# One written-out order of all five engines replaced by another in a kernel of chunk-selecting attention and a gated MLP

## The chip, the core and the metric

The kernel runs on one core of a Trainium2 chip. The metric is the device time of one execution in microseconds (us). A core has TensorE (PE: products into PSUM, one queue of weight loads and products), VectorE (DVE), ScalarE (ACT), GpSimd (POOL) and SyncE (SP); here POOL issues the loads from memory and SP issues the transfers inside the core and the stores. All of them run at once and meet only at semaphores; each works through its own instructions in the order in which they were written.

## What is computed

Four batches of eight heads, 768 positions, 64 numbers a head. Keys are cut into 24 chunks of 32 positions; a query attends to the six chunks whose bound (from the chunk's smallest and largest key) is highest.

```
ub = sum(max(q*k_min, q*k_max))            # per query and chunk, causal
sel = the 6 chunks with the largest ub
attn = softmax(scale * q @ k.T, where sel and j <= i)
x = (attn @ v), heads side by side         # 4 x 768 x 512
h = relu(x @ w_in);  u, v = halves of h
v_n = (v - mean) / sqrt(var + 1e-6)
out = (u * (w_spatial @ v_n + b_spatial)) @ w_out
```

## The kernel before

**Pairs.** The work of the attention is cut into 16 pairs of heads, four to a batch; two pairs share one group g of loads. For pair i the operations carry these names: `lk`, `lq`, `lv` (POOL starts the loads of keys, queries and values, L598, L604, L609; for group 0 in quarters, L613), `kT` (six TensorE transposes of the keys, L674), `kmax`, `kmin` (DVE, chunk bounds, L698), `kb` (L725), `qT` (five transposes of the queries, L739), `rq` (positive and negative parts, L748, L750; the very first on ACT, L745), `ub` (bounds on TensorE, L756, L759), `top` (ten maxima on DVE, L769), `sel` (which chunks fall out, L795; it writes into the query tile `qs`, beside the queries, whose other columns were zeroed by `ring`, L541). The query tile is then transposed into the tile `a`: for pairs 0 to 7 on TensorE (`aT`, L802 and L814, with copies `ac`, L807 to L817), for pairs 8 to 15 by a DMA transpose that SP issues (`aTd`, L820). The tile `kh` holds the transposed keys and the matrix that spreads a chunk's mask over its 32 positions (`kh`, L583); `kop` brings the keys there: copies on ACT or DVE for pairs 0 to 7 (L734), DMAs issued by SP for pairs 8 to 15 (L732), one for each head of the pair; `kc` (L720) is the copy out of PSUM before them. `kop91` is thus the DMA for the second head of pair 9.

**Scores to output.** `sc` (scores, six groups of up to 512 columns for each head, L827), `ex` (exponential on ACT, L836), `tri` (the causal triangle on POOL for batches 1 to 3, L842), `av` (L853), `rc` and `nm` (division, L858, L863), then the transpose of the result `x` into the layout of the MLP: through TensorE (`xp`, L878, and a copy, L881) for pairs 0 to 3 and 15, by an SP DMA transpose (L872) for the others. `sc901` is pair 9, first head, group 1; `sc914` pair 9, second head, group 4.

**MLP.** For each batch and each of six blocks of 128 positions: `v` and `u` (products with `w_in`), `va`, `bs`, `vs`, `rs`, `vn` (normalising), `s` (product with `w_spatial`), `gt` (L994), `gd` (DMA transpose of the gated block by SP, L1009; the last two through TensorE, L1001), `o` (product with `w_out`), `oc` (copy, L1014), `os` (store by SP, L1018). All these products are line L951. Those of one batch are put between the pairs of the next.

**Zero products.** `dm` (L889) multiplies a tile of zeros: 42 products at the start, then single ones (`dm0` to `dm64`) placed among the first pairs.

**What sets the order.** A planner in the file (`build`, L171) knows each operation's engine, duration, inputs and buffers. What it found was written into the file as one string `ORDER` (L393 to L465) of 1452 names; the kernel walks through it (L1054) and emits each operation on its engine. So the order on each engine is the order of the names of that engine's operations, and nothing is rearranged later. `PLAN` (L391) holds the counts of buffers, the number of zero products and a list `flip` of the copies that change between ACT and DVE. A semaphore wait stands on the instruction that needs the data, and whatever follows it on that engine waits too. POOL's DMAs share eight semaphores in turn, SP's another eight, so that a DMA isn't issued before the one eight places earlier has landed.

**Counting a place.** TensorE starts a 128-column product 0.056 us after the one before it, a 512-column one 0.216 us after (104 of them in a row took 22.48 us in the chain of waits). With every product counted at such a spacing and without the zero products, the kernel has 177.0 us of TensorE work; "the place" of a name is the work that stands ahead of it in `ORDER`. The first scores are at place 3.2, the first product of the MLP (`v00.0`) at 32.7.

Of the kernel before, what the change touches and what calls it, by code (L numbers as in the profile page):

```python
# [166 lines left out]
def mmc(n): return max(n/2.4+2.5,25)/1000  # L167
DEF=dict(BEATS=12,pa=8,dve_a=(),qx=('ACT',),xp=4,mlp_first=13,mlp_mul=1.0,sc=3,tr=1,acc=1,ml=3,kbuf=3,qbuf=3,vbuf=3,ebuf=3,late=240,chunk=2,
  lk=40,lq=36,lv=18,kdma=99,kcp=2,kcdma=1,kc_act=(),shift=4,prep=0.0,tm=.8,lm=0.2,lm2=1.2,gp=(),head=1,lag=0.0,kp=27,ca=99,tree=0,svk=1.48,svh=.96,svw=1.15,flip=(),wide=0,pt=(),kdm=0,xd=(),dum=0,dum0=42,split=1,warm0=0.,qa_dve=(),ma_act=(),mkbuf=2)
PEL=0.2  # L170
def build(prm=None):  # L171
# [8 lines left out]
    for i in range(p['qbuf']): op(f'ring{i}','DVE',.81,.05,deps=['id0'],prio=B0 if i==0 else B0+.9)  # L180
# [210 lines left out]
PLAN = {'late': 40, 'mlp_first': 8, 'qbuf': 5, 'kbuf': 6, 'vbuf': 6, 'dum': 65, 'warm0': 5.3, 'kcp': 8, 'flip': ['ac10', 'ac41', 'ac51', 'ac60', 'ac71', 'gd34', 'kc10', 'kc12', 'kc13', 'kc9', 'kh00', 'kh11', 'kop00', 'kop40', 'kop71', 'oc01', 'oc03', 'oc13', 'oc21'], 'gp': ((3, 4), (3, 5)), 'lm': 0.2, 'lm2': 1.2, 'tm': 0.8, 'dum0': 42, 'split': 1}  # L391

ORDER = """  # L393
dz id0 dm ring3 lk010 ring2 lk000 ring0 lq010 id1 lq000 expand lk001 kh00 kh30 ring4 lk011 kT0 kh21 ring1 mlat dm0
kTb0 lq011 dm1 kh11 dm2 dm3 dm4 dm5 kop01 dm6 dm7 kmin0 dm8 dm9 dm10 dm11 lq001 qTb0 kh31 qT0 kmax0 dm12 lk11 dm13
dm14 dm15 dm16 dm17 dm18 dm19 dm20 rq01 dm21 dm22 dm23 dm24 small dm25 dm26 dm27 dm28 dm29 dm30 lk10 kh20 kb0 kT1 rq00
kop00 ub0 kh01 lv0 dm31 dm32 kmax1 kTb1 dm33 dm34 kop11 qT1 top00 lq10 dm35 dm36 dm37 dm38 dm39 kmin1 dm40 dm41 kop10
dm42 dm43 dm44 dm45 dm46 dm47 dm48 dm49 dm50 dm51 mtri dm52 dm53 dm54 selA0 dm55 kh10 top01 aTA00 lq11 dm56 kb1 dm57
dm58 dm59 sel0 rq11 aTB0 dm60 rq10 dm61 dm62 dm63 dm64 wsp0 acA00 ub1 win00 acB0 sc000 top10 sc001 lk20 ex000 aTA01
top11 sc002 ex001 acA01 sc005 kT2 lk21 sel1 ex002 sc004 kop20 ex005 sc013 ex004 lq20 sc011 kmin2 ex013 aT10 sc003  # L400
ex011 sc010 ac10 lq21 av000 ex003 kop21 aT11 ex010 sc015 av001 lv1 sc100 kmax2 ex015 av002 ac11 sc012 rc00 kb2 ex012
qT2 nm00 sc102 lk31 ex100 kT3 rq21 av010 ex102 rq20 sc014 win21 kmax3 sc112 ex014 ub2 win11 sc101 ex112 kmin3 sc104
qT3 ex101 sc111 av011 ex104 top20 lk30 sc105 av012 ex111 kb3 sc103 top21 ex105 rc01 sc113 sel2 ex103 rq31 wsp4 aT20
ex113 rq30 sc115 sc114 ac20 nm01 ub3 kop30 ex114 av100 win01 sc201 ex115 top30 av101 ex201 sc203 kop31 av102 sc110
ex203 lv2 top31 ex110 aT21 rc10 sel3 kT4 ac21 nm10 qT4 sc200 kmin4 sc205 sc202 ex200 aT30 kmax4 ex202 sc215 av110
ex205 ex215 wsp5 av111 rq40 kop40 sc211 av112 kb4 rq41 sc204 sc212 ex211 rc11 kop41 ub4 lq30 aT31 ac30 sc210 top40 kT5
ex204 nm11 xp0 lq31 ex212 top41 av200 kop50 ac31 sc213 win30 av201 sel4 ex210 av202 sc214 kmax5 qT5 ex213 win20 sc300
ex214 xp1 rc20 rq51 sc301 ex300 sc310 nm20 win31 ex301 rq50 av210 ex310 kmin5 sc311 win10 av211 sc303 ex311 sc302 x1
av212 ex303 sc304 kop51 aT40 ex302 rc21 ex304 kb5 kT6 nm21 sc305 ac40 sc315 sc313 kmin6 av300 ex305 wsp1 aT41 ex315
ex313 x0 sc404 sc312 ac41 ex404 sc314 lk40 av301 kmax6 ex312 ub5 sc401 ex314 av302 sc400 top50 xp2 ex401 rc30 sc403  # L410
wsp2 top51 ex400 sc402 sel5 ex403 nm30 aT50 ex402 sc415 kop61 av310 lq40 ac50 av311 x2 sc412 ex415 av312 kop60 sc405
qT6 ex412 sc411 ex405 kT7 rc31 ex411 nm31 sc501 tri40 sc413 rq61 ex501 sc414 xp3 rq60 wsp3 ex413 kmax7 aT51 ex414
av400 sc502 kb6 sc410 kop71 x3 sc500 av401 ac51 v00.0 ex410 kmin7 av402 ex502 v00.2 tri41 ub6 ex500 kop70 sc504 sc503
lq41 sc505 top60 ex503 v02.0 top61 v04.0 ex504 lk41 rc40 v02.2 sel6 va00 nm40 sc510 qT7 va02 lk51 v04.2 ex510 rq71
sc513 kb7 av410 rq70 ex513 lq61 v01.0 bs02 av411 ex505 aT60 va04 bs00 v01.2 tri50 av412 ac60 sc514 va01 v03.0 lv3 rc41
vs02 nm41 sc603 ub7 ex603 bs01 v03.2 x4 sc511 ex514 lb top70 wsT0 ex511 av500 vs01 top71 sc512 lv4 va03 sc515 av501
sel7 wsT1 ex515 wsc0 sc600 ex512 av502 vs00 aT61 wsc1 ex600 v05.0 lq50 rc50 ac61 nm50 kT8 sc601 v05.2 kmax8 lq51 ex601
aT70 va05 sc604 kmin8 av510 lk61 ac70 sc613 sc602 u01.0 kc8 ex604 tri51 qT8 bs05 ex613 av511 wsT2 lk50 ex602 kb8 u01.2
rq80 sc611 rq81 u00.0 ex611 bs03 sc610 aT71 ua01 wsc2 av512 u00.2 ex610 vs05 bs04 sc704 wsT5 ua00 u02.0 vs04 ex704
ac71 wsT4 vs03 rc51 u02.2 rs0 nm51 sc605 sc614 wsc5 ub8 ex605 x5 ex614 sc612 wsc4 tri60 av600 ua02 sc700 vn00 av601  # L420
wsT3 ex612 vn04 sc701 ex700 u04.0 top80 av602 wsc3 sc703 u03.0 vn01 ex703 sc615 u04.2 rc60 ex701 nm60 u03.2 ua04 u05.0
top81 ua03 av610 sel8 sc702 vn03 ex615 sc710 aTd8 kT9 ex702 vn02 tri61 sc712 ex710 av611 kmin9 s00.0 lk60 ex712 u05.2
kop80 kmax9 av612 kop81 sc715 sc705 ua05 s00.2 wout1 rc61 ex715 qT9 vn05 kc9 sc711 s01.0 nm61 ex705 sc714 kop91 kb9
s00.4 rq91 tri70 x6 av700 rq90 s01.2 gt00 sc713 s02.0 ex713 gd00 av701 ub9 ex714 kT10 top90 s01.4 ex711 kop90 s02.2
top91 tri71 sc802 sel9 sc800 gt01 sc801 ex802 aTd9 av702 wout3 s02.4 ex801 rc70 wout2 s03.0 nm70 ex800 sc804 gt02 qT10
gd01 ex804 av710 kmax10 sc803 sc805 av711 sc810 ex803 s04.0 gd02 kmin10 ex805 av712 ex810 sc815 s03.2 tri80 ex815 rc71
sc812 kb10 kc10 nm71 s03.4 wout0 s04.2 ex812 x7 gt03 lv7 kT11 sc813 rq100 av800 ex813 sc811 rq101 gd03 av801 s05.0
kmax11 ex811 sc814 av802 s05.2 ex814 kop101 rc80 kmin11 s04.4 sc905 sc901 ub10 ex905 nm80 ex901 sc904 s05.4 kb11 gt04
ex904 sc900 av810 ex900 kc11 sc911 sc903 o01.0 ex911 top100 sc915 o00.0 top101 ex915 ex903 sc902 sel10 av811 o01.2
ex902 gt05 aTd10 qT11 sc910 oc01 tri90 v10.0 rq110 o00.2 tri81 kop100 rq111 sc914 v10.2 oc00 gd04 v11.0 lq60 ex914  # L430
ub11 ex910 av812 v11.2 gd05 lv5 va10 rc81 o02.0 nm81 va11 v13.0 top110 o02.2 kop110 top111 lq71 v14.0 sel11 oc02 sc912
bs10 av900 ex912 sc913 kT12 ex913 aTd11 v13.2 kmax12 v14.2 tri91 va13 av901 sc1000 kmin12 va14 sc1002 lk71 av902
ex1000 sc1012 v12.0 rc90 ex1002 nm90 o03.0 lk70 ex1012 bs11 sc1004 sc1005 av910 ex1004 bs14 qT12 av911 ex1005 o03.2
kc12 vs14 vs11 v12.2 oc03 sc1010 kop121 v15.0 va12 rq121 x8 av912 sc1003 sc1001 rc91 bs12 u10.0 ex1001 v15.2 rq120
os02 ex1010 u11.0 nm91 kop120 va15 u10.2 vs10 kop111 bs13 av1000 ua10 u11.2 os01 bs15 o04.0 ex1003 x9 kb12 kT13 ua11
vs13 tri100 o04.2 kmax13 sc1015 sc1014 oc04 sc1013 av1001 ub12 vs12 ex1014 kmin13 av1002 o05.0 ex1015 ex1013 sc1101
top120 u12.0 kc13 vs15 sc1011 rc100 top121 sc1104 ex1101 o05.2 kop130 sel12 ex1011 u13.0 nm100 os00 qT13 ex1104 kop131
tri101 u12.2 rq131 rs1 sc1100 aTd12 av1010 oc05 lv6 vn10 sc1103 sc1102 ua12 vn11 u13.2 ex1103 vn13 av1011 u14.0 ua13
vn14 u15.0 ex1100 rq130 av1012 u14.2 kb13 ex1102 rc101 vn15 u15.2 ua14 vn12 s10.0 ua15 sc1114 ub13 s10.2 top130 sc1110
sc1105 s10.4 nm101 ex1105 ex1110 s11.0 tri110 gt10 kT14 ex1114 s11.2 kmin14 lq70 gd10 s12.0 av1100 kmax14 sc1115 s11.4  # L440
ex1115 s12.2 gt11 sc1113 av1101 s12.4 kc14 gd11 sc1112 s14.0 gt12 ex1112 sc1111 av1102 top131 ex1113 s13.0 gd12 rc110
sel13 ex1111 s15.0 nm110 s14.2 tri111 sc1203 aTd13 sc1200 s14.4 ex1203 av1110 ex1200 gt14 s13.2 x10 av1111 sc1213
av1112 sc1201 ex1213 kT15 rc111 nm111 sc1202 s13.4 kmax15 ex1202 x11 sc1205 s15.2 ex1201 qT14 gt13 s15.4 ex1205 sc1215
kc15 sc1204 o10.0 ex1204 rq140 sc1210 kop151 av1200 gt15 ex1215 o10.2 os05 tri120 av1201 kb14 os03 rq141 sc1212 oc10
sc1302 kmin15 o12.0 gd13 ex1210 av1202 ex1212 ub14 rc120 sc1300 nm120 o12.2 gd15 ex1300 top140 sc1214 v21.0 ex1302
top141 v20.0 oc12 sel14 sc1310 ex1214 v21.2 sc1211 ex1310 qT15 sc1313 aTd14 ex1211 sc1303 rq150 v20.2 va21 rq151
tri121 av1210 ex1313 kb15 o11.0 gd14 ex1303 ub15 v23.0 va20 top150 av1211 sc1314 kop150 top151 sc1311 av1212 ex1314
# [638 lines left out]
```

## Time and profile before

| | |
|---|---|
| runs | 202.15, 202.21, 202.73 us; median 202.21 |
| the profiled execution | 202.94 us by its own clock; its span, first to last instruction, 201.2 us |
| busy: PE, DVE, ACT, POOL | 191.0, 158.5, 147.3, 79.7 us |
| products | 2058, of them 107 zero products |
| POOL's DMA queue | 76,544 packets, 12.20 MB, 90.5% of 16 engines' span |
| SP's DMA queue | 38,192 packets, 16.06 MB, 39.1% |
| first scores product | 16.38 us |
| first product of the MLP | 50.98 us |
| last product of TensorE starts | 197.08 us |

A busy PE isn't a PE at its peak, since the ends of its products are modelled; its waits are read from the distance between starts. The chain of waits follows the work that ended last back to the start. The view of instructions in order of time names, in square brackets, an engine's idle time before an instruction and what ended it.

### The profile page before, as it was taken

Reading aid. Unit: us, or ns where it says so; the run is one execution under the profiler, and the core shown is the slowest. Engines: PE = TensorE matmul, PEld = TensorE weight load, DVE = VectorE, ACT = ScalarE, POOL = GpSimd, SP = SyncE. Lnnn points to the kernel's source line nnn. Section 1 sums busy time; section 2 is a strip of 40 time slices with the busy share of each in tenths; the row PEclk is TensorE's granted clock in tenths of the full one; section 3 lists DMA queues with packets and bytes.
Section 4 is the critical chain, followed back from the end, with each engine's and each line's share of the span. In section 5 each row is a group of like instructions: output and inputs, shape, how many; then the busy total and the mean of one; then the engine's idle time right before and its main releaser. Section 6 shows DMA issues by size and latency. Waiting matters only on the chain.

```text
span 201.2 us, 5310 instructions
## 1 busy us (share of the span) xinstructions
PE 191.0 (95%) x2058; PEld 121.3 (60%) x2058; DVE 158.5 (79%) x477; ACT 147.3 (73%) x295; POOL 79.7 (40%) x96
## 2 busy tenths in 40 slices
PE   7859999999999999999999999999999999999992
PEld 7747777776577766555656655656555555444451
DVE  5998999999999999999598999697378337257430
ACT  2956999999989886767897973589889751664151
POOL 7999957442699224452851412111112130000000
PEclk9999999999999999999999999999999999999998
DMA  6999999999599999999999999786673265342335
GB/s 42 94 123 160 166 161 180 172 192 73 56 147 132 143 123 142 176 161 176 198 128 171 227 219 135 145 215 108 217 119 42 78 119 136 126 175 90 78 127 212
DMA packets 114761, 28.60 MB, mean 142 GB/s; under 512 B 108720, under 2 KB 111280, under 8 KB 114736
## 3 DMA queue, kind: packets, MB, share of 16 engines
q0 software_dynamic: 76544, 12.20, 90.5%
q1 hardware_dynamic: 38192, 16.06, 39.1%
q8 instruction: 16, 0.26, 0.6%
q14 instruction: 9, 0.07, 0.1%
HBM read 24.38 MB, written 6.29 MB: 152 GB/s over the span
## 4 chain that ended last, share of the span: by engine, by line
PE 69%; DVE 14%; DMA 8%; POOL 3%; ACT 2%; issue 2%; POOLq 0%; ACTq 0%; DVEq 0%
PE mlp L951 40%; PE sc L827 12%; PE acc L853 8%; DMA a<-qs 4%; DVE kmm L698 3%; DMA qs<-in_q_dram 3%; DVE vn L988 2%; DVE max L769 2%; POOL k L613 2%; DVE kh L734 2%; PE trq L739 2%; PE tra L814 1%; PE ub L759 1%; PE kTp L674 1%; DVE x L863 1%
## 5 line engine op out<-in xcount | busy, mean ns | idle before, releaser
L836 ACT ACTIVATE e<-sc 128x512 f16<-128x512 f32 (+1 forms) x192 | 93.8, 565 | 19.9 <-PE sc L827 15.2
L827 PE MATMUL sc<-a,kh 128*128 128x512 f16 (+3 forms) x256 | 61.2, 305 | 0.6 <-DMA a<-qs 0.3
L951 PE MATMUL mlp<-w_in_sb,xT 128*128 128x512 f16 x192 | 52.2, 379 | 0.0
L842 POOL TENSOR_SCALAR_AFFINE_SELECT e<-e 128x768 f16<-128x768 f16 x24 | 20.9, 874 | 75.7 <-ACT e L836 62.8
L853 PEld LDWEIGHTS <-e 128*128 128x128 f16 x672 | 31.4, 97 | 14.5 <-DVE x L863 0.5
L951 PE MATMUL mlp<-vn,wsT 128*128 128x512 f16 x144 | 38.8, 379 | 0.1
L853 PE MATMUL acc<-vt,e 128*128 128x65 f16 x672 | 35.8, 193 | 0.1
L698 DVE TENSOR_REDUCE kmm<-kTp 128x24 f16<-128x768 f16 x32 | 29.6, 946 | 1.3 <-PE kTp L674 1.2
L827 PEld LDWEIGHTS <-kh 128*128 128x128 f16 x256 | 22.5, 97 | 13.1 <-issue 0.8
L951 PE MATMUL mlp<-w_out_sb,gT 128*128 128x512 f16 x92 | 26.1, 379 | 0.0
L951 PEld LDWEIGHTS <-xT 128*128 128x128 f16 x192 | 17.2, 98 | 14.3 <-issue 0.2
L994 DVE SCALAR_TENSOR_TENSOR g<-mlp,b_col,u 128x512 f16<-128x512 f32 x24 | 17.9, 747 | 9.3 <-PE mlp L951 7.3
L1014 ACT COPY o<-mlp 128x512 f32<-128x512 f32 x19 | 11.1, 589 | 16.9 <-PE mlp L951 16.5
L973 DVE BATCH_NORM_STATS2 stats<-vraw 128x6 f32<-128x512 f32 x24 | 15.9, 677 | 5.8 <-ACT vraw L968 5.8
L951 PEld LDWEIGHTS <-wsT 128*128 128x128 f16 x144 | 12.7, 97 | 10.3 <-issue 0.2
L863 DVE TENSOR_TENSOR x<-acc,rec 128x384 f16<-128x384 f32 x32 | 17.6, 551 | 0.6
L983 ACT ACTIVATE u<-mlp 128x512 f16<-128x512 f32 x24 | 14.0, 597 | 4.8 <-PE mlp L951 4.1
L769 DVE MAX8 max<-ub 128x8 f32<-128x8 f32 (+4 forms) x160 | 15.2, 163 | 1.2 <-PE ub L759 1.0
L968 ACT ACTIVATE vraw<-mlp 128x512 f32<-128x512 f32 x24 | 14.2, 608 | 2.4 <-PE mlp L951 2.4
L604 POOL DMA_DIRECT2D qs<-in_q_dram x14 | 14.5, 1044 | 2.4 <-DMA qs<-in_q_dram 1.6
L598 POOL DMA_DIRECT2D k<-in_k_dram x14 | 14.6, 1047 | 0.9 <-DMA ws_raw<-in_moe_w_spatial_dram 0.4
L988 DVE TENSOR_SCALAR vn<-vraw,mv,rstd 128x512 f16<-128x512 f32 x24 | 13.6, 621 | 0.8 <-ACT rstd L1024 0.6
(83 smaller groups left out, 233.6 us busy)
## 6 DMA issues: line engine op xcount, KB each, us to landing
out_dram<-o SPq DMA_DIRECT2D x23, 256.0 KB, 2.3
vt<-in_v_dram POOLq DMA_DIRECT2D x8, 384.0 KB, 9.2
k<-in_k_dram POOLq DMA_DIRECT2D x14, 192.0 KB, 7.9
qs<-in_q_dram POOLq DMA_DIRECT2D x14, 192.0 KB, 7.9
kh<-kT SPq DMA_DIRECT2D x16, 96.0 KB, 4.5
ws_raw<-in_moe_w_spatial_dram POOLq DMA_DIRECT2D x6, 192.0 KB, 6.8
w_in_sb<-in_moe_w_in_dram POOLq DMA_DIRECT2D x8, 128.0 KB, 8.5
w_out_sb<-in_moe_w_out_dram POOLq DMA_DIRECT2D x4, 128.0 KB, 5.0
```

Of the source, the lines that this page charges most:

```text
L598: nc.gpsimd.dma_start(out=k_tile(g)[:, :, :, hi, :].rearrange("p x t d -> p (x t) d"), in_=source(k, b, 2 * hp + 2 * hi, 2))
L698: nc.vector.tensor_reduce(self.kmm[:, m, :], src, axis=AX.X, op=op, negate=(m == 1))
L769: nc.vector.max(self.max8[:, qi - 1, hi, :], self.ub[:, c0:c0 + CPT * (qi + 1)])
L827: mm(sc[:, col:col + n], lhsT=self.kh[hi][:, t * P:(t + 1) * P], rhs=self.a[:, q0 // P:(q0 + n) // P, hi, :], start=True, stop=not diag)
L836: nc.scalar.activation(out=self.e[hi][:, g * 512:g * 512 + width], in_=self.sc[hi, g][:, 0:width], func=Act.Exp, scale=scale)
L842: nc.gpsimd.affine_select(out=blk, in_=blk, compare_op=Alu.is_ge, fill=0.0, base=0, channel_multiplier=-1, pattern=[[0, NQT], [1, P]])
L853: mm(self.av[hi][:, qi, :], lhsT=self.e[hi][:, c:c + P], rhs=self.v[hi][:, t, 0:D + 1], start=first and n == 0, stop=last and n == len(blo ...
L863: nc.vector.tensor_tensor(self.x16[:, :, hi, :], in0=self.av[hi][:, :, 0:D], in1=self.rec[hi].to_broadcast([P, NQT, D]), op=Alu.mult)
L951: mm(st[kind, ti], lhsT=lhsT, rhs=rhs, start=(j == 0), stop=(j == n - 1))
L973: nc.vector.bn_stats(st["stats", ti], st["vraw"][:, ti, :])
L988: nc.vector.tensor_scalar(vn[:, ti, :], in0=st["vraw"][:, ti, :], scalar1=st["mv"][:, ti, 0:1], scalar2=st["rstd"][:, ti, :], op0=Alu.subt ...
L994: nc.vector.scalar_tensor_tensor(g, in0=st["s", ti], scalar=b_col[:, ti:ti + 1], in1=st["u"][:, ti, :], op0=Alu.add, op1=Alu.mult)
```

## The change

The string `ORDER` is replaced as a whole: the same operations in another order, apart from six zero products fewer and some copies that change engine. `PLAN`:

```diff
-'dum': 65
+'dum': 59
-'flip': ['ac10', 'ac41', 'ac51', 'ac60', 'ac71', 'gd34', 'kc10', 'kc12', 'kc13', 'kc9', 'kh00', 'kh11', 'kop00', 'kop40', 'kop71', 'oc01', 'oc03', 'oc13', 'oc21']
+'flip': ['ac10', 'ac31', 'ac41', 'ac51', 'ac60', 'ac71', 'kc10', 'kc11', 'kc13', 'kc9', 'kh00', 'kh10', 'kh11', 'kop31', 'kop40', 'kop50', 'kop71', 'oc00', 'oc01', 'oc03', 'oc11', 'oc21', 'oc25']
```

From ACT to DVE go `kh10`, `ac31`, `oc00`, `oc11`, `oc25`, `kc12` and the copy `gd34`; from DVE to ACT go `kop00`, `kop31`, `kop50`, `kc11`, `oc13`.

The start of the order:

```diff
-dz id0 dm ring3 lk010 ring2 lk000 ring0 lq010 id1 lq000 expand lk001 kh00 kh30 ring4 lk011 kT0 kh21 ring1 mlat dm0
-kTb0 lq011 dm1 kh11 dm2 dm3 dm4 dm5 kop01 dm6 dm7 kmin0 dm8 dm9 dm10 dm11 lq001 qTb0 kh31 qT0 kmax0 dm12 lk11 dm13
+dz id0 dm small lk010 ring1 lk000 ring3 lq000 ring2 lq010 ring4 id1 lk011 expand lk001 ring0 kT0 kh01 lq001 dm0 kh11
+kTb0 kh20 kmax0 dm1 dm2 dm3 dm4 dm5 dm6 lq011 dm7 dm8 dm9 dm10 dm11 kop00 kmin0 qT0 mlat qTb0 dm12 lk11 dm13 dm14 dm15
```

DVE's instructions up to the choice of pair 1, before and after (the zero products, spread between them, left out):

```
before  dz id0 ring3 ring2 ring0 expand kh00 ring4 ring1 kh11 kmin0 kmax0 small kb0 rq00 kop00 kmax1 top00
        kmin1 selA0 top01 kb1 sel0 rq11 rq10 acA00 acB0 top10 top11 acA01 sel1
after   dz id0 small ring1 ring3 ring2 ring4 expand ring0 kh11 kmax0 kmin0 rq00 kb0 kh10 kh00 top00 selA0 top01
        kmin1 kmax1 sel0 rq10 rq11 acA00 kb1 acB0 acA01 top10 top11 sel1
```

SP's instructions up to pair 11's transpose, before and after:

```
before  x4 x5 aTd8 kop80 kop81 kop91 x6 gd00 kop90 aTd9 gd01 gd02 x7 gd03 kop101 aTd10 kop100 gd04 gd05 kop110 aTd11
after   x4 aTd8 kop80 x5 kop81 gd00 kop90 aTd9 x6 gd01 kop91 gd02 x7 kop111 gd03 gd05 kop100 aTd10 kop101 gd04 kop110 aTd11
```

POOL's loads from the second group on, in part:

```
before  lk11 lk10 lv0 lq10 mtri lq11 wsp0 win00 lk20 lk21 lq20 lq21 lv1 lk31 win21 win11 lk30 wsp4 win01 lv2 ...
after   lk11 lk10 lv0 lq10 mtri lq11 win10 win31 win20 lk20 win30 lk21 lq20 lq21 win11 lv1 win01 win21 lk30 lb lk31 ...
```

Of the 63 loads, 23 stand more than 1 us of TensorE work earlier (`wout1` 34, `lq70` 22, four of `win` 14 to 19, `lv6` 13) and 19 more than 1 us later (`wsp0` 24, `win00` 19, `lq50` 11, `lv2` 7). At the end SP issues the stores `os23`, `os24`, `os25` after the last transposes `gd30` to `gd33` instead of before them.

In the code, `ring` may now be done by POOL or ACT; `PLAN` gives neither, so the five memsets stay on DVE.

```diff
-        act(f"ring{i}")(lambda i=i: nc.vector.memset(qs_ring[i][:, :, :, 0:4:3, :], 0.0))
+        empty = qs_ring[i].rearrange("p x t s d -> p (x t) s d")[:, :, 0:4:3, :]
...
+            eng = nc.gpsimd if i in prm["rpool"] else nc.vector
+            act(f"ring{i}")(lambda empty=empty, eng=eng: eng.memset(empty, 0.0))
```

## The prediction

> **What bounds the kernel.** I read the slices of the page first, then busy times by stage, then the head in order of time, then SP's queue. The page:
>
> ```profile
> PE   7859999999999999999999999999999999999992
> ...
> DMA  6999999999599999999999999786673265342335
> ```
>
> TensorE is full but for the start, and the DMA engines are full from 5 to 50 us and from 55 to 125 us. By stage:
>
> ```profile
> 4.30:16.40 12.10, 8.78 (x149) 7.89 (x147) 11.13 (x40) 7.95 (x10) 11.95 (x17) 1.00 1.79 115
> 16.40:50.00 33.60, 32.18 (x500) 24.98 (x496) 32.91 (x112) 32.45 (x68) 20.46 (x26) 1.00 1.86 159
> 50.00:80.00 30.00, 30.00 (x374) 19.97 (x372) 29.33 (x92) 25.61 (x54) 18.46 (x19) 1.00 1.97 121
> 80.00:126.00 46.00, 45.53 (x469) 26.92 (x466) 40.66 (x125) 34.63 (x72) 18.20 (x20) 1.00 1.69 176
> ```
>
> The columns are the stretch, its length, then PE, PEld, DVE, ACT, POOL busy. Up to 50 us DVE is the bound (11.13 of 12.10, 32.91 of 33.60), ACT close behind (32.45). From 51 us, when the first MLP product can start, TensorE always has something ready and is the bound. With each product at its spacing, 144.2 us of work stand behind `v00.0`; it starts at 50.98 and the last product starts at 197.1: 1.9 us of waits in 146. Before that, between the first scores (16.38) and `v00.0`, 29.6 us of work take 34.6: 5.0 us of waits. So the order can win in two places, the start of the MLP and the few waits behind it; and it can lose wherever a transfer comes later than TensorE reaches its user, since nothing behind it on TensorE can pass.
>
> **The head.** In order of time:
>
> ```profile
> 4.35 0.55 DVE L559 TENSOR_SCALAR expand<-identity 64x768 f16<-64x768 f16 x1 [0.85 <-POOL identity L538]
> ...
> 13.71 0.44 PE L739 MATMUL trq<-identity,qs 128*128 128x128 f16 x5 [1.88 <-DMA qs<-in_q_dram]
> ...
> 15.58 0.42 DVE L807 COPY a<-trp 128x512 f16<-128x512 f16 x1 [0.42 <-PE trp L802]
> ...
> 21.96 0.44 PE L739 MATMUL trq<-identity,qs 128*128 128x128 f16 x5 [0.26 <-DMA qs<-in_q_dram]
> ```
>
> DVE idles 0.85 us for the identity, and 0.42 and 0.13 us near the end. After the change `small` (9.30 to 10.05, 0.75 us) and four memsets (0.81 each) fill DVE until 5.07; POOL makes the identity after four loads, at 1.32 + 0.95 + 3 x 0.85 + 0.34 = 5.2; `expand` follows without a wait. From 5.2 DVE does `expand` 0.98, a memset 0.8, `kh11` 0.35, two reductions 1.82, `rq00` 0.48, `kb0` 0.2, two copies 0.7: 10.5; `top00`, `selA0`, `top01` 1.2; two reductions 1.9; `sel0` 0.25, both `rq` 0.9, the first `a` copy 0.4: 15.1. TensorE's first scores go from 16.38 to about 15.2, 1.2 earlier. The second quarter of the queries is issued 0.65 us earlier (before, it landed at the end of a 5.08 us piece of the chain, at 13.57); `rq10` now wants it at 13.7, so it costs 0 to 0.3 even if it lands no sooner. Six zero products fewer are 6 x 0.056 = 0.34 us of TensorE in time that was idle anyway: nothing. The granted clock (the column behind POOL) is 1.00 through a wait of 1.88 us before; the longest that I expect after, from the last zero product ahead of pair 1's queries to their landing, is about the same, so the clock should hold.
>
> **Up to `v00.0`.** DVE's work ahead of `x3`, on which `v00.0` waits, loses `kop00`, `kop31`, `kop50` (0.55 each) and gains `kh10` (0.35) and `ac31` (0.55): -0.75. ACT, from its first exponential on, gains two `kop` (0.80 each) and loses `ac31` (0.83): +0.77 against a start 1.2 earlier. But the queries of pair 2 land by POOL's queue, which has been full since 3 us and has the same loads ahead of them; TensorE waited for them at 21.96 and will again. DVE reaches their `rq` at 22.1 to 22.3 instead of 22.52, so most of the 1.2 is lost there. What is left is 0.2 to 0.4 there and 0.3 to 0.6 of the work that leaves DVE: I take **-0.7** for `v00.0`. Bounds: 0 (ACT or the loads take the rest as well) and -1.8 (1.2 kept, and 0.6 of the work).
>
> **Loads.** Behind 22 us no product waits for a load in the view of waits, so issuing them early pays nothing by itself. Four `win` now stand ahead of group 2; each takes the queue about 0.9 us, and `wsp0`, `win00` (2.0 together) go: +1.5 for the keys of pair 4, which had landed 4.2 us before their use. Nothing is late. The cover is gone only if the queue loses 2 us more.
>
> **SP's queue.** This is the part that I charge. Before:
>
> ```profile
> 76.90 1.86 SPq L732 DMA_DIRECT2D kh<-kT  x3
> 78.80 1.32 SPq L872 DMA_TRANSPOSE xT<-x  x1
> 80.16 1.27 SPq L1009 DMA_TRANSPOSE gT<-g  x1
> 81.48 0.59 SPq L732 DMA_DIRECT2D kh<-kT  x1
> 82.18 1.84 SPq L820 DMA_TRANSPOSE a<-qs  x1
> 84.13 3.35 SPq L1009 DMA_TRANSPOSE gT<-g  x2
> ```
>
> and on TensorE, where pair 9's first scores waited for that `a`:
>
> ```profile
> 90.32 0.43 PE L827 MATMUL sc<-a,kh 128*128 128x128 f16 x2 [0.32 <-DMA a<-qs]
> ```
>
> The transposes issued from 84 to 91 us took, from issue to landing, 8.0 (`a`, 82.18 to 90.19 in the chain), 6.1 (`gT`) and 8.2 (`xT`), while POOL's weights were loading. From 130 to 150 us, with no load about, the same kinds took 4.4, 2.4 and 3.2, and `kh` 2.2:
>
> ```profile
> kh<-kT SPq DMA_DIRECT2D x4, 96.0 KB, 2.2
> gT<-g SPq DMA_TRANSPOSE x3, 2.4
> xT<-x SPq DMA_TRANSPOSE x2, 3.2
> a<-qs SPq DMA_TRANSPOSE x2, 4.4
> ```
>
> Before, `kop91` was the last of the three at 76.90, ahead of the jam, with 13.3 us of TensorE work between its place and its user. Now it stands behind `aTd9`, `x6` and `gd01`: some 1.8 + 1.3 + 1.7 us of issue later than `aTd9`, and 4.4 us of TensorE work (place 67.0 to 71.4) ahead of `sc914`. Transfers of that place took 6.1. It would be 6.1 - 4.4 = 1.7 late; 0 by the quiet 2.2; 3.8 by `xT`'s 8.2. I take 1.7, because the nearest rows in time and queue are the two `gT` behind the same `a`. Pair 9's `a` has 7.8 us of work before its user instead of 7.6 and was 0.48 late between starts (0.32 in the row): 0.3 remains. Together 2.0 in place of 0.48: **+1.5**, bounds -0.5 and +3.6. Pair 11's `a` has 8.7 instead of 11.0 and came 1.6 early; `kop101` 5.9 instead of 12.0: 0 after a wait at pair 9, up to +1.0 without it. `kop80`, just in time before, has 1.6 more.
>
> The Trainium skill, "DMA: Bandwidth & Descriptors", section "Queues, rings and completion order", says that each DMA engine takes turns between queues packet by packet and starts descriptors of one ring in order. By it `kop91` can't overtake `aTd9`, and every load issued early takes turns from SP's transposes; without it the 2.2 us row would hold and this part would cost nothing.
>
> **The rest.** The other waits behind 51 us (1.9 - 0.48 = 1.4 us, none over 0.3) change places: 0, bounds -0.7 and +1.0. The stores `os23` to `os25` move from 178 us to about 192 us; stores in a row landed some 0.65 us apart, and the copies that need their buffers come 1.5 us and more behind: 0, or 0.65 for each that is late.
>
> **Sum.** -0.7 + 1.5 = +0.8 on the profiled execution's 202.94 (201.2 of span and 1.7 around it): 203.7. The median of the runs is 0.73 below that execution; on it, **203.0 us**. About 0.3%, 0.6 us, is what a measurement of this kernel tells from no change.
>
> **Rivals.**
> - *The queue keeps up* (0.33). SP issues `aTd8` earlier (place 54.0 instead of 55.9) and so may enter the jam ahead of time; `kop91` then lands in 4.4. The head's gain stands and pair 9's wait goes: -0.7 to -1.2, 201.3. It decides if `kop91` lands within 4.4 us of its issue.
> - *Both, about equal* (0.20). `kop91` 0.7 late, or the head's 0.7 gone with the loads and no wait at pair 9: 202.2.
> - *The order doesn't do what it is for*: 19 of 63 loads stand later, `lq50` by 11 us. Before, none of these was waited for; it is part of the second rival.
> - The forecast's case (0.47): 202.5 to 204.6.
>
> Faster by over 0.3%: 0.27 of the first rival and 0.04 of the second, 0.31. Within: 0.06 + 0.12 + 0.07 = 0.25. Slower: 0.40 + 0.04 = 0.44. The range, 201.0 to 204.5, leaves out a full head gain of 1.8 with no wait, and two late pairs together.
>
> **What will show it.** First scores at 15.2, not 16.4. `v00.0` near 50.3. A row of `sc` with a wait "<-DMA kh<-kT" near 90 us of 1 to 2 us; if there is none, the queue kept up. The place of 177.0 us of work doesn't change, so the span's change must equal that of `v00.0` plus that of the waits behind. I am wrong in kind if DVE waits in the head for the later identity, or if waits come up in pairs 10 to 15.

## The result, and the profile after

| | kernel before | changed kernel |
|---|---|---|
| runs | 202.15 to 202.74 us, median 202.47 | 206.88 to 210.56 us, median 208.41 |
| ratio, 95% interval | | 1.027 [1.020, 1.034]: slower |
| span of the profiled execution | 201.2 us | 208.9 us (210.56 by its own clock) |
| first scores product | 16.38 us | 14.77 us |
| `v00.0` | 50.98 us | 49.89 us |
| from `v00.0` to the last product's start | 146.1 us | 154.8 us |

The head won 1.1 us at `v00.0` (0.7 forecast); behind it the kernel lost 8.7 us in this execution. The profiled execution is the slowest of the four: the ratio goes by the other three, which took 206.88 to 208.93 us at mean granted clocks of 0.991, 0.989 and 1.000 against its 0.982. (Lines of the changed file stand 6 lower: L827 is now L833, L951 is L957.) The slices of the page after the change:

```profile
PE   7979999899999989969997799999999999999992
...
PEclk9999999999999999988999699999999999999999
DMA  6999999999999198998999994397659194500575
```

TensorE has two dents in its full stretch, at 89 to 94 and at 110 to 120 us (each slice is 5.2 us), the granted clock, which had none before the end, dips twice, and the DMA engines have a hole in slice 14 (68 to 73 us). The busy times of the stage in which the loss lies, with the columns as before:

```profile
80.00:126.00 46.00, 41.16 (x399) 23.85 (x397) 32.55 (x104) 30.56 (x62) 17.73 (x19) 0.93 1.57 151
```

PE was busy 45.53 of the 46.00 us from 80 to 126 and now is 41.16, at a mean clock of 0.93. The head in order of time, the rows that answer those of before:

```profile
5.17 0.55 DVE L565 TENSOR_SCALAR expand<-identity 64x768 f16<-64x768 f16 x1 [0.17 <-POOL identity L538]
```

```profile
12.70 0.44 PE L745 MATMUL trq<-identity,qs 128*128 128x128 f16 x5 [1.29 <-DMA qs<-in_q_dram]
...
21.02 0.72 PE L745 MATMUL trq<-identity,qs 128*128 128x128 f16 x10 [0.21 <-DMA qs<-in_q_dram]
```

The later identity costs DVE 0.17 us instead of 0.85, and pair 2's queries are again waited for, 0.9 us earlier. Now pair 9, TensorE in order of time:

```profile
89.03 0.59 PE L957 MATMUL mlp<-vn,wsT 128*128 128x512 f16 x2
89.47 0.35 PE L859 MATMUL acc<-vt,e 128*128 128x65 f16 x6
89.66 0.38 PE L833 MATMUL sc<-a,kh 128*128 128x256 f16 x2
92.08 0.53 PE L833 MATMUL sc<-a,kh 128*128 128x256 f16 x2 [2.04 <-DMA kh<-kT]
92.40 1.06 PE L957 MATMUL mlp<-vn,wsT 128*128 128x512 f16 x2
```

The row at 92.08 is `sc914`, waiting for `kop91`. Behind it the same pair of 512-column products that took 0.59 us at 89.03 takes 1.06. At pair 11:

```profile
113.33 0.44 PE L859 MATMUL acc<-vt,e 128*128 128x65 f16 x9
116.13 0.58 PE L833 MATMUL sc<-a,kh 128*128 128x256 f16 x2 [2.36 <-DMA a<-qs]
116.51 1.06 PE L957 MATMUL mlp<-w_out_sb,gT 128*128 128x512 f16 x2
```

By the distance between starts the two waits are 2.20 and 2.52 us. The clock (last but two of the columns) stretch by stretch around the first and the second:

```profile
88.70:92.10 3.40, 1.36 (x14) 0.61 (x13) 2.43 (x6) 1.73 (x4) 0.86 (x1) 1.00 1.02 103
92.20:95.60 3.40, 3.40 (x30) 2.07 (x29) 0.31 (x1) 1.69 (x4) 0.00 (x0) 0.50 2.37 185
95.70:99.10 3.40, 3.27 (x30) 1.79 (x28) 3.37 (x16) 1.36 (x3) 2.50 (x3) 1.00 0.51 102
...
116.10:119.50 3.40, 3.37 (x15) 1.57 (x15) 0.05 (x1) 1.18 (x2) 0.00 (x0) 0.50 1.57 207
```

In this execution each of the two waits is followed by 3.41 us at half the clock, which costs 1.7 us of work. The loss behind `v00.0` adds up: 2.20 + 2.52 for the two waits, 3.4 for the clock, 0.70 at `s00.0` (for a copy of `wsT`), 0.45 for `kop101`, 0.29, 0.20 and 0.32 at three other places: 10.1, less the 1.9 us of waits that there were before: 8.2 of the 8.7. DVE between the two waits:

```profile
91.77 0.75 DVE L1000 SCALAR_TENSOR_TENSOR g<-mlp,b_col,u 128x512 f16<-128x512 f32 x1 [0.97 <-DMA gT<-g]
95.70 0.75 DVE L1000 SCALAR_TENSOR_TENSOR g<-mlp,b_col,u 128x512 f16<-128x512 f32 x1 [3.18 <-DMA gT<-g]
96.36 0.90 DVE L775 MAX8 max<-ub 128x8 f32<-128x8 f32 x10
97.30 0.41 DVE L801 TENSOR_TENSOR qs<-ub,max 128x240 f16<-128x240 f32 x1
```

This is `gt04`, the last of the gated blocks, waiting for the transfer `gd02` that reads the buffer it writes to (three buffers of `g`, L999); behind it stand pair 10's maxima and choice, and SP can't issue pair 10's transpose before them. SP's queue shows it:

```profile
84.85 1.23 SPq L1015 DMA_TRANSPOSE gT<-g  x1
86.13 0.59 SPq L738 DMA_DIRECT2D kh<-kT  x1
86.81 2.49 SPq L1015 DMA_TRANSPOSE gT<-g  x1
...
97.78 1.79 SPq L826 DMA_TRANSPOSE a<-qs  x1
...
104.15 4.05 SPq L826 DMA_TRANSPOSE a<-qs  x1
```

`kop91` (86.13) stands between `gd01` and `gd02`; it landed at 92.03, `gd02` at 95.60, pair 10's `a` (97.78) at 104.59, pair 11's (104.15) at 116.09, 11.9 us after its issue.

### The profile page after: what moved, and what is told of

The parts are those of the page before. It is cut to its first block, busy times and chain, and to the rows that moved or that the text cites. A ratio compares the mean times of both kernels' runs of the same rounds, so it can differ in the third digit from the quotient of the medians.

```text
span 208.9 us, 5294 instructions
## 1 busy us (share of the span) xinstructions
PE 194.9 (93%) x2052; PEld 123.3 (59%) x2052; DVE 157.9 (76%) x479; ACT 148.6 (71%) x293; POOL 79.3 (38%) x96
## 4 chain that ended last, share of the span: by engine, by line
PE 57%; DMA 15%; ACT 11%; DVE 6%; POOL 5%; issue 2%; SPq 0%; POOLq 0%; DVEq 0%; ACTq 0%
PE mlp L957 36%; PE sc L833 9%; ACT e L842 8%; PE acc L859 6%; DMA a<-qs 6%; DMA gT<-g 4%; DMA qs<-in_q_dram 3%; DMA kh<-kT 2%; DVE vn L994 2%; ACT a L823 2%; PE trq L745 2%; POOL k L619 2%; POOL qs L619 1%; ACT kh L740 1%; PE kTp L680 1%
## 5 line engine op out<-in xcount | busy, mean ns | idle before, releaser
L842 ACT ACTIVATE e<-sc 128x512 f16<-128x512 f32 (+1 forms) x192 | 95.1, 556 | 24.3 <-PE sc L833 21.2
L833 PE MATMUL sc<-a,kh 128*128 128x512 f16 (+3 forms) x256 | 64.3, 312 | 5.7 <-DMA a<-qs 2.4
L957 PE MATMUL mlp<-w_in_sb,xT 128*128 128x512 f16 x192 | 52.9, 379 | 0.2 <-ACT u L989 0.2
L957 PE MATMUL mlp<-vn,wsT 128*128 128x512 f16 x144 | 40.0, 383 | 0.5 <-DVE wsT L651 0.5
L859 PE MATMUL acc<-vt,e 128*128 128x65 f16 x672 | 36.3, 195 | 0.1
L833 PEld LDWEIGHTS <-kh 128*128 128x128 f16 x256 | 23.2, 98 | 20.0 <-issue 3.2
L957 PE MATMUL mlp<-w_out_sb,gT 128*128 128x512 f16 x92 | 27.2, 391 | 0.0
L957 PEld LDWEIGHTS <-xT 128*128 128x128 f16 x192 | 17.4, 98 | 15.3 <-issue 0.4
L1020 ACT COPY o<-mlp 128x512 f32<-128x512 f32 x17 | 10.0, 589 | 12.8 <-PE mlp L957 12.7
L957 PEld LDWEIGHTS <-wsT 128*128 128x128 f16 x144 | 12.2, 98 | 10.0 <-DVE wsT L651 1.0
```

The lines of the kernel that those rows point to most:

```text
L833: mm(sc[:, col:col + n], lhsT=self.kh[hi][:, t * P:(t + 1) * P], rhs=self.a[:, q0 // P:(q0 + n) // P, hi, :], start=True, stop=not diag)
L842: nc.scalar.activation(out=self.e[hi][:, g * 512:g * 512 + width], in_=self.sc[hi, g][:, 0:width], func=Act.Exp, scale=scale)
L859: mm(self.av[hi][:, qi, :], lhsT=self.e[hi][:, c:c + P], rhs=self.v[hi][:, t, 0:D + 1], start=first and n == 0, stop=last and n == len(blo ...
L957: mm(st[kind, ti], lhsT=lhsT, rhs=rhs, start=(j == 0), stop=(j == n - 1))
```

## The experiments

Of each kernel the ratio to the kernel before, run beside it on the same chip, is given. Most only move names in `ORDER`. e2 adds zero products and e16 leaves some out; e7, e9 and e10, which join the head of one kernel to the rest of the other, and e15, which is built on e7, take for each part the zero products and the copies' engines (`flip`) of the kernel that it comes from.

### First theories: places on SP's queue, or the clock, or the last loads

POOL's last seven loads now stand in a row ahead of `tri91`:

```
before  lq60 lv5 lq71 tri91 lk71 lk70 tri100 tri101 lv6 tri110 lq70
after   lq60 lk71 lv5 lq70 lk70 lq71 lv6 tri91 tri100 tri101 tri110
```

**e1**, SP's queue:

```diff
-... kop81 gd00 kop90 aTd9 x6 gd01 kop91 gd02 ...
+... kop81 kop91 gd00 kop90 aTd9 x6 gd01 gd02 ...
```

> The changed kernel with one name moved: kop91 on SP from behind gd01 to ahead of gd00 (behind kop81), as the kernel before had it ahead of that pair's transpose. Theory A (the order on SP's queue makes each late transfer by itself; a wait of over 2 us also halves the clock for 3.4 us): the wait of 2.20 us at pair 9's second head goes, and the half-speed stretch behind it (1.7 us); pair 11's wait stays as it is: 208.4 - 3.9 = 204.5 us, between 204 and 205. Theory B (SP's and POOL's transfers share full DMA engines, so what is won at pair 9 is only waited for at pair 11): pair 11's wait grows from 2.5 to 4.5 us or more and the time stays above 206.5 us.

Ratio 1.016 [1.005, 1.027]. The wait for `kop91` is gone (it landed at 81.29), but pair 10 now waits for its `a` and for `kop101`, as the view of waits says:

```profile
PE sc L833 <- DMA a<-qs: 2.1, 1, 2.1
PE sc L833 <- DMA kh<-kT: 2.0, 1, 2.0
```

Between starts 2.27 and 2.16 us, with one half-speed stretch. Theory A falls by the trace, B has its point: the wait only moved, though to pair 10 and not to 11. The ratio, which lies between the two cases, doesn't decide.

**e2**, two fills in `scores`:

```diff
+            for _ in range(FILL.get((self.i, hi, g), 0)):
+                mm(sc[:, 0:P], lhsT=idle_op, rhs=idle_op, start=True, stop=True)
+FILL = {(9, 1, 4): 38, (11, 0, 4): 42}
```

> The changed kernel with 38 zero products (128 columns, 0.056 us each, 2.1 us) ahead of the first product that needs kop91 and 42 (2.35 us) ahead of the first that needs pair 11's transpose; nothing else moves. Theory A with the clock as a cost of its own: TensorE waits as long as before but at work, the clock stays at 1.00, and the two half-speed stretches of 3.41 us go: about 3.4 us less, 205.0 us, between 204.3 and 206. Theory C (the clock falls for another reason, or the half-speed stretches cost nothing because the transfers behind them are late too): 208 us or more, since what is put in can only add.

The clock stayed at 1.00 from 3.9 us to the end of the work, and no half-speed product is left behind the waits; from `v00.0` to the last product the profiled execution took 152.9 us, 1.9 less than the changed kernel's 154.8, but 1.0 more than the 151.8 of e11 below, which is the changed kernel again and whose clock didn't dip either, without a fill. The ratio is 1.029 [1.018, 1.040], and the 3.4 us forecast, a ratio of about 1.009 to 1.017, lie outside it. That the fill held the clock, this profile alone can't tell; what the clock follows, the last section shows. The 3.4 us didn't appear, and the transfers are no earlier: the fill ahead of `sc914` still left 0.7 us of wait, and pair 10 waited 0.61 and 0.67 us.

**e3**, `lv6` behind `tri101` and `lq70` behind `tri110`, and **e4**, the same and e1's move.

> The changed kernel with two of POOL's loads moved back to where the kernel before has them: lv6 behind tri101 and lq70 behind tri110, which takes them (1.3 MB with the others of that burst becomes less) out of the seven loads issued between 97 and 105 us. Theory B: pair 11's transpose no longer shares the engines with them and lands earlier than 116.1 us on the trace's time line; its wait of 2.52 us shrinks to under 1 us and the second half-speed stretch goes: 208.4 - 1.5 - 1.7 = about 205 us. Theory A: these loads stand mostly behind that transpose, its flight of 7.9 us from the end of its issue stays, and the time stays within 207.5 to 209.

> Both moves together: kop91 ahead of gd00 and the two loads back. If the two late transfers are separate, their gains add: Theory A without B gives 204.5, with B for pair 11 about 201.5 us (208.4 - 3.9 - 3.2 = 201.3). If the DMA engines are the bound anyway, the time stays above 205 us.

e3: 1.031 [1.019, 1.042]; e4: 1.029 [1.020, 1.039]. In e4 pair 11's `a` landed at 112.38, 10.8 us after its issue, against 12.7 in e1, which differs by these two loads alone, so they do delay it; but TensorE waited 1.90 us for pair 10's choice, 1.66 for its `a` and 2.32 for `kop101`, and pair 14's queries, now loaded too late, were waited for 1.02 us more. Neither was a fair trial of B: the five loads that are issued first stayed together.

### Whole stretches, and the burst

**e5**, the last loads in the order `lq60 lv5 lq71 tri91 lk71 lk70 tri100 tri101 lv6 lq70 tri110`; **e6**, the same with e1's move.

> The changed kernel with six of POOL's last seven loads spread as in the kernel before: lv5 and lq71 behind lq60, lk71 and lk70 behind tri91, lv6 and lq70 behind tri101, instead of all seven in a row before tri91. kop91 stays late. Theory B (loads put early take turns with SP's transposes on full DMA engines): pair 9's wait of 2.2 us and its half-speed stretch stay, but pair 11's wait (2.5 us) and the stretch behind it (1.7 us) go: about 4 us less than the changed kernel, ratio to the kernel before about 1.005 to 1.012. Theory A (places on SP's queue alone): no change, ratio 1.02 or more.

> The same with kop91 ahead of gd00 as well. Theory B: both losses go and the head's 1.1 us stays: 201 to 202.5 us, ratio 0.995 to 1.003. If pair 10's transpose is still late, because pair 9 without its wait brings the loads and the transposes to the engines 2 us sooner (as in the run with kop91 alone, where pair 10 waited 2.3 and 2.2 us), the ratio is above 1.01 and the bound is the DMA engines, not two places in the order.

e5: 1.019 [1.012, 1.025], above B's 1.005 to 1.012. In the profile it went as B said: pair 11's `a` landed at 111.56 without a wait and without the second dip; pair 9's wait (2.89 us) and its dip stayed. e6: 1.023 [1.015, 1.032]; pair 9's wait went and pair 10's `a` was late:

```profile
102.00 0.34 PE L859 MATMUL acc<-vt,e 128*128 128x65 f16 x6
105.47 1.01 PE L833 MATMUL sc<-a,kh 128*128 128x512 f16 x3 [3.13 <-DMA a<-qs]
```

**e7**, the changed order up to `v00.0`, then the old; **e8**, the old kernel with the burst.

> The order of the changed kernel up to v00.0, then that of the kernel before (lq40, which only the latter had issued by then, put in at the seam; lb, lk41, lq41 and wout1 left out behind it, since they are issued already). The first product of the MLP starts 1.1 us earlier as in the changed kernel. If what stands behind it keeps pace: 1.1 us less than the kernel before, ratio 0.994 to 0.996. If the DMA engines set the pace from 55 to 125 us, pair 9 and pair 11 wait for the 1.1 us and the ratio is 1.000; above 1.003 would mean that the kernel before stood just at the edge and that any earlier start costs.

> The kernel before with one thing done to it: the loads lk71, lv5, lq70, lk70, lq71 and lv6 in a row behind lq60, ahead of tri91, as the changed kernel has them. Theory B: pair 11's transpose, which landed 1.6 us ahead of its use, comes 2 to 5 us later; a wait of 1 to 4 us appears ahead of pair 11's first scores, with a half-speed stretch if it is over 2 us: ratio 1.005 to 1.025. Theory A: nothing changes, ratio 1.000 plus or minus 0.003.

e7: **0.990 [0.986, 0.994]**, eight runs from 200.87 to 201.79 us: better than both kernels. `v00.0` starts at 49.66, and 145.7 us follow to the last product's start, with no wait over 0.3. So the changed head is a gain, and the loss lies wholly behind `v00.0`. e8: 1.011 [1.006, 1.017]; its profile doesn't show the wait that B named (pair 11's `a` landed at 111.71, its first product came at 112.50), only a dip of the clock in the head, where no load was moved: `v00.0` starts at 51.82, 0.8 us later than before, and that is most of the 1.1 us that this execution, the second fastest of ten, is longer. Its ratio speaks for B, its trace doesn't.

**e9**, the changed order up to pair 9's choice (80 us), then the old; **e10**, the old head and the changed rest; **e11**, the changed kernel again.

> The order of the changed kernel up to pair 9's choice of chunks (some 80 us), then that of the kernel before; kop91, x6, av701, s02.2 and tri71, which only the latter had issued by then, stand at the seam. If the loss lies wholly in the order from pair 9 on (where kop91 stands, and where the last loads stand against the transposes of pairs 9 to 11), this keeps the head's gain less the 0.7 us wait at s00.0: 201.2 to 202.2 us on a chip where the head alone took 201.2, ratio 0.990 to 0.997. If the part between 51 and 80 us already spoils what follows, the ratio is above 1.003.

> The reverse of the head alone: the order of the kernel before up to v00.0, then that of the changed kernel (lb, lk41, lq41 and wout1 at the seam). If the loss is in the rest by itself: v00.0 at 51 us, the waits at pair 9 and at pairs 10 or 11, ratio 1.02 to 1.035, 1.1 to 1.5 us more than the changed kernel. If the loss comes only because the earlier head brings pair 9 into the jam of the loads sooner, the waits shrink by the 1.1 us each and the ratio is 1.01 or less.

> The changed kernel itself beside the others on this chip: ratio 1.027 as before, within 1.020 to 1.034, with the two waits of 2 to 3 us ahead of sc914 and of pair 11's first scores, each with 3.4 us at half the clock behind it.

e9: 1.004 [1.000, 1.009]; e10: 1.015 [1.009, 1.021]; e11: 1.026 [1.020, 1.032]. Against e7's 0.990 (another chip), the order from 51 to 80 us costs some 1.4%, what follows 2.2% more. e10 lies between its two cases: the rest loses by itself, and its ratio is lower than e11's although it lacks the changed head; its profile can't say why, since `v00.0` started at 50.04 there, hardly later than with the changed head. In e11's profile the clock didn't dip, though the wait for `kop91` was 2.52 us; the last section comes back to that. So e11 shows the loss without the clock: 151.8 us from `v00.0` to the last product, 5.7 more than before, with waits between starts of 2.52 for `kop91`, 1.44 for `kop101` and 1.00 for pair 11's `a` (the rows below), 0.70 at `s00.0` and 0.52 for pair 10's choice.

```profile
93.20 0.39 PE L833 MATMUL sc<-a,kh 128*128 128x256 f16 x2 [2.35 <-DMA kh<-kT]
...
106.61 0.39 PE L833 MATMUL sc<-a,kh 128*128 128x512 f16 x1 [1.28 <-DMA kh<-kT]
...
115.36 0.38 PE L833 MATMUL sc<-a,kh 128*128 128x256 f16 x2 [0.84 <-DMA a<-qs]
```

**e12**, as e6, but of the burst only `lq60` ahead of `tri91`: `lq60 tri91 lv5 lk71 lk70 tri100 lq71 tri101 lv6 lq70`.

> kop91 ahead of gd00, and of the burst of loads only lq60 ahead of tri91: lv5, lk71 and lk70 behind it, lq71 behind tri100, lv6 and lq70 behind tri101. If the 3.3 us wait for pair 10's transpose in the run with kop91 and the spread burst came from lv5 and lq71 standing on the engines ahead of it (landed 106.67 and 108.46 us there, the transpose 105.43), that transpose lands by 101 us, no wait of over 1 us is left, and the ratio is 0.992 to 1.002. If pair 10 still waits 2 us or more, it isn't the loads that hold it, and the DMAs that SP itself issues ahead of it (kop111, gd05 and gd03, moved forward by the change) are the next suspect: ratio 1.012 or more.

1.015 [1.009, 1.021]. Pair 10's transpose landed at 101.30, about as said, and pair 11's at 105.87 (116.09 in the changed kernel). But now `lv5` itself was late:

```profile
110.70 0.38 PE L833 MATMUL sc<-a,kh 128*128 128x384 f16 x2
115.05 0.65 PE L859 MATMUL acc<-vt,e 128*128 128x65 f16 x9 [3.96 <-DMA vt<-in_v_dram]
```

So loads and transposes do delay each other, and from 74 to 116 us the DMA engines have no time for both.

### The gap

The loads that POOL issues between the triangles, changed kernel:

```profile
58.61 1.48 POOL L615 DMA_DIRECT2D vt<-in_v_dram  x1
61.59 0.86 POOL L848 TENSOR_SCALAR_AFFINE_SELECT e<-e 128x768 f16<-128x768 f16 x1 [1.50 <-issue]
66.73 0.86 POOL L848 TENSOR_SCALAR_AFFINE_SELECT e<-e 128x768 f16<-128x768 f16 x1 [4.28 <-ACT e L842]
70.77 0.86 POOL L848 TENSOR_SCALAR_AFFINE_SELECT e<-e 128x768 f16<-128x768 f16 x1 [3.18 <-ACT e L842]
71.58 1.03 POOL L610 DMA_DIRECT2D qs<-in_q_dram  x1
```

From 60 to 71.6 us POOL issues nothing, for `lq50` (71.58) stands behind three triangles, the last two of which wait for exponentials. The DMA view of 64 to 76 us, in slices of 0.3 us, of the changed kernel:

```profile
DMA  9999999999211000000000000003999997199999
```

The engines stand idle for 4.0 us (68.3 to 72.3), right ahead of the stretch in which they have no time. e9, with the changed order up to 80 us alone, has the gap too, 3.5 us from 68.5 on: there `gd01` and `gd02` land at 91.97 and 95.91 (in e7 at 87.95 and 90.53), `gt04` and `gt05` wait for them on DVE, and TensorE waits 1.80 and 1.73 us for those two. **e13** fills the gap: `lq50 lk60 wout3 wout2 wout0` directly behind `lv4`. **e14** does this, e1's move and e5's.

> The changed kernel with five loads moved on POOL: lq50 and lk60 from behind tri61, wout3, wout2 and wout0 from behind tri70 to tri80, all to directly behind lv4 (issued at 60 us). In every profile of the changed kernel POOL issues nothing from 60 to 71.5 us, and the DMA engines fall idle around 68 to 73 us; then they are full until 125. Theory D (a queue of work: what isn't moved in that gap is waited for later by pair 9 to 11): 5 us of transfers leave the full stretch, the transposes from 74 us on land 1 to 4 us earlier, the wait for kop91 falls from 2.5 us to under 1, pairs 10 and 11 under 1 in all: ratio 1.000 to 1.010. Theory A (places on SP's queue alone) and the burst (seven last loads in a row): no change up to pair 11, ratio 1.018 to 1.03.

> The same five loads, kop91 ahead of gd00, and the last loads spread as in the kernel before. Theory D: no wait of over 1 us is left behind v00.0, the head's 1.1 us stay: ratio 0.990 to 1.000. If pair 10's transpose is late again by 3 us, the gap isn't what filled the engines there: ratio 1.01 or more.

e13's engines in the same slices:

```profile
DMA  9999999999999999999999981039999999889953
```

`kop91`, in its late place, landed at 87.85 instead of 92.03 and nothing waited for it: half of theory D. But the ratio is 1.027 [1.021, 1.033]: TensorE waited 1.77 us for pair 10's choice, 1.08 for its `a` and 2.70 for `kop101`. e14: **0.993 [0.988, 0.998]**. One wait of over 0.5 us is left, 1.63 for `kop101`. The gap decides between e6 (1.023) and e14, yet does nothing by itself.

**e15** moves `lq50` and `lk61` of e7 behind `tri61`; **e16** is e7 without its 59 single zero products.

> The kernel with the changed head and the rest of the kernel before, and two loads in it, lq50 and lk61, moved from 59 and 61 us to behind tri61 (about 74 us), where the changed kernel has lq50 and lk60. Theory D: the DMA engines idle for some 2.5 us near 66 to 71 us, and pair 9's transpose, which landed just in time, comes 1 to 2.5 us late: ratio 0.995 to 1.010 instead of 0.990. If the gap is harmless: 0.988 to 0.993.

> The same kernel with the changed head, without its 59 single zero products (the 42 at the start stay). If they hold the granted clock in the head: the clock falls to half between 10 and 20 us for one or more stretches of 3.41 us, the transposes and bounds ahead of the first scores take twice as long, first scores 0.3 to 1 us later and v00.0 0.3 to 1.5 us later, ratio 0.992 to 1.000. If they do nothing for it: the same as with them, ratio 0.990.

e15: 1.000 [0.996, 1.004], instead of 0.990 (on another chip): two loads 15 us later cost 1%, and pair 9's `a` came 1.82 us late. e16: 1.004 [1.001, 1.008], above both cases. The clock dipped in the head, first scores at 14.84 (14.77 with them), `v00.0` at 50.83 (50.37 in e15, on the same chip):

```profile
4.10:14.20 10.10, 4.76 (x74) 3.78 (x71) 9.76 (x28) 7.74 (x10) 9.89 (x15) 1.00 1.71 110
14.30:17.70 3.40, 3.26 (x29) 2.44 (x30) 2.57 (x16) 1.77 (x4) 3.40 (x5) 0.50 2.28 144
17.80:21.20 3.40, 3.34 (x53) 2.69 (x51) 3.18 (x5) 3.13 (x8) 2.63 (x4) 1.00 1.80 180
```

So the zero products hold the clock, and not in the profiled executions alone: the mean granted clock of e16's ten runs was 0.975 to 0.992, that of e15's ten and e7's eight 0.995 to 1.000. What that is worth at `v00.0` isn't shown: with its zero products the same head started it anywhere from 49.58 (e4) to 50.70 (e11). That e16 lost 3 us more behind `v00.0` than e7, in the same order, isn't explained.

### What is left of kop91

**e17** is e14 with `kop91` in its late place; **e18** is e14 with `kop101` ahead of pair 10's `a`, behind `gd03`.

> The changed kernel with the gap filled and the last loads spread, but kop91 left where the change put it. If kop91's place costs only because the engines were full (in e13 it landed at 87.9 us instead of 92.0, with no wait), this equals e14: ratio 0.989 to 0.997. If its place costs by itself: a wait of 1 us or more ahead of sc914 and a ratio above 1.000.

> e14 (gap filled, kop91 early, last loads spread) with kop101 moved from behind pair 10's transpose to ahead of it (behind gd03, where the kernel before has it). Its wait of 1.63 us, the only one of e14's profile over 0.5 us, goes: 1.0 to 1.6 us less than e14, ratio 0.983 to 0.989. If only the wait moves to pair 10's transpose: ratio 0.990 to 0.996.

e17: 1.022 [1.015, 1.028], which neither case foresaw: no wait for `kop91`, yet all of the loss. The two traces differ in one name, and DVE tells why. e17:

```profile
90.06 0.73 DVE L1000 SCALAR_TENSOR_TENSOR g<-mlp,b_col,u 128x512 f16<-128x512 f32 x1
92.71 0.75 DVE L1000 SCALAR_TENSOR_TENSOR g<-mlp,b_col,u 128x512 f16<-128x512 f32 x1 [1.92 <-DMA gT<-g]
93.38 0.90 DVE L775 MAX8 max<-ub 128x8 f32<-128x8 f32 x10
94.31 0.41 DVE L801 TENSOR_TENSOR qs<-ub,max 128x240 f16<-128x240 f32 x1
```

e14:

```profile
90.10 1.39 DVE L1000 SCALAR_TENSOR_TENSOR g<-mlp,b_col,u 128x512 f16<-128x512 f32 x2
91.42 0.90 DVE L775 MAX8 max<-ub 128x8 f32<-128x8 f32 x10
92.35 0.41 DVE L801 TENSOR_TENSOR qs<-ub,max 128x240 f16<-128x240 f32 x1
```

With `kop91` ahead of it, `gd02` lands at 92.62 instead of 90.21; `gt04` waits for it on DVE, pair 10's choice ends 2 us later, and SP issues pair 10's `a` at 94.80 instead of 92.86. POOL, which waits for none of this, issues `lq60` and `lv5` at 93.1 and 94.2 in both. In e14 the `a` is ahead of `lq60` and lands at 99.85; in e17 it is behind and lands at 104.20. All profiles agree:

| pair 10's `a` issued, against `lq60` | kernels | issue to landing |
|---|---|---|
| 1.0 to 2.9 us ahead | before, e7 to e10, e15, e16 | 3.8 to 6.1 us |
| 0.3 ahead to 0.4 behind | after, e2, e5, e11, e14, e18 | 5.7 to 7.8 us |
| 1.1 to 1.8 us behind, `lv5` 1 to 2 us after `lq60` | e1, e3, e4, e6, e13, e17 | 8.2 to 10.5 us |
| 1.9 us behind, `lv5` 10 us later | e12 | 5.5 us |

The old order has `gt04` as the fifth block, not the sixth: it takes the buffer of `gd01`, and `gt05`, which takes that of `gd02`, stands behind the choice. The changed order swaps the two and puts both ahead of the choice. In twelve of the fourteen profiles with the changed rest, all but e14's and e18's, `gt04` starts 0.1 us after `gd02` lands. Moving `gt04` behind the choice, the direct test, wasn't tried.

e18: 0.996 [0.992, 0.999]. `kop101` is on time, and pair 11's `a` waits 2.14 us instead, with a dip: once more the wait moved. e7 has the lowest ratio of all, though its interval overlaps e14's.

## Why the prediction was wrong

It said 203.0 us in a range of 201.0 to 204.5, and was measured at 208.41.

- **The head** was right, and undersized. First scores at 14.77 (15.2 forecast), `v00.0` at 49.89 (50.3): 1.1 us instead of 0.7 (one execution of each; in the others' profiles the old head gives 50.04 and 51.82, the changed one with its zero products 49.58 to 50.70). As forecast, the rest of the 1.6 went at pair 2's queries. e7 has it as 1.0% of the time.
- **The clock** held through the head, as said. The prediction had no price for a clock that falls behind its own waits, and no case of its range has the 3.4 us that this took of the profiled execution. But the loss doesn't hang on it: e11's profiled execution, without such a dip, took 208.38 us, and the changed kernel's run with a mean clock of 1.000 took 208.93.
- **kop91** was sized well: 6.1 us of flight forecast, 5.9 from issue to landing measured; 1.7 us late forecast, 2.20 measured (6.1 and 2.52 in e11). Pair 9's `a` was not 0.3 late but 2.9 us early, for it was issued 1 us sooner and landed in 4.8.
- **Loads.** "Nothing is late" is a step that failed. It asked of each load whether its own user waits, saw that none does, and put `lq50`, 11 us later, into a rival as harmless. What a late load costs is the time of the engines it takes later from others: e15 prices two such loads at 1%, e13 gives `kop91` 4.2 us back.
- **Pair 11's `a` and `kop101`**, "0 after a wait at pair 9", is the step that failed most: 2.52 us with a dip and 0.45 us in the profiled execution; 1.00 and 1.44 in e11, and 0.52 for pair 10's choice. It took the distance to the user in TensorE's work and let the wait at pair 9 count as time won. But the same late transfers hold DVE too, by `gd02` and `gt04`, and so what stands behind it, pair 10's choice first, while POOL's loads don't wait and go first. Of DVE's order behind 51 us the prediction looked at nothing.
- **The rest**, 0 with bounds of -0.7 and +1.0, had 0.70 at `s00.0` alone.
- The prediction named waits in pairs 10 to 15 as what would make it wrong in kind. That is what came. The rule of the Trainium skill that it weighed ("DMA: Bandwidth & Descriptors", "Queues, rings and completion order": queues take turns packet by packet, one ring starts in order) agrees with e12 and with the table above, as far as SP's and POOL's transfers delay each other; that they take turns by the packet, no run here shows. A start in order doesn't by itself say that `kop91` can't land ahead of `aTd9`; here it landed 6.1 us behind it (92.03 against 85.92). The mistake was to apply the rule to one transfer.

What stays open: e10's place between its cases, where e8 loses its 1.1%, e16's 3 us behind `v00.0`, and, until `gt04` is moved by itself, how much of the loss goes through DVE.

## What to carry to other kernels

Where the DMA engines are full, a load has no price of its own: count the work that stands ahead of each transfer that something waits for, and ask whether an idle stretch of the engines comes before it. Before charging one late transfer, follow every in-order engine that waits for it or for what stands behind it, since a queue that doesn't wait will pass the one that does. When mending one wait only moves it, look for the shared resource, and mend several places at once.

## What the runs showed of the hardware

The clock was granted in windows of 3.413 us (every stretch at full clock in the 20 profiles is a multiple of it: 85.33, 102.40, 109.23 us). I added up TensorE's idle time in each window at full clock up to 195 us, over 1,000 of them, with each product counted at its spacing: behind all 14 with 2.14 us or more idle, the next window ran at half; behind none with 1.98 us or less. So what a wait does to the clock depends on where it falls. The changed kernel's 2.20 us lay wholly in the window from 88.78 to 92.19; e11's 2.52 us lay across a border, 1.69 of them in one window, and the stretch behind it ran at full clock:

```profile
89.70:93.10 3.40, 1.14 (x12) 0.51 (x10) 2.40 (x6) 1.54 (x3) 0.86 (x1) 1.00 1.73 119
93.20:96.60 3.40, 3.40 (x42) 2.13 (x43) 1.31 (x9) 2.34 (x5) 0.29 (x1) 1.00 2.49 179
```

A window at half with 1.25 to 1.94 us idle was followed by another at half, in five cases (e3, e4, e6, e12, e13); each of the 14 with 0.27 or less by one at full clock. The Trainium skill ("TensorE: Matmul & The Clock Gate", "What's actually happening") has the window run free, which fits the borders found here, and lets the clock fall after one or more idle windows of about 3.4 us. Here 2.14 us idle in a window, 63% of it, was enough. In the profile of the kernel before, one window of the head stood at 1.90 us idle, just below the edge; in e8, with the same head, one had 2.47, and the clock dipped. With the changed head no window ahead of the first scores had more than 1.63, and without its zero products (e16) one had 2.68.
